# Four more row groups turned by VectorE in a linear-attention and mixture-of-experts kernel

## The chip, the cores and the metric

The kernel runs on one core of a Trainium2 chip. The metric is the device time of one execution in microseconds (us); the number to compare is the median of several runs. The core has a matrix engine (TensorE, PE in the profile; its weight loads are listed as PEld), a vector engine (VectorE, DVE), an activation engine (ScalarE, ACT), GpSimd (POOL) and SyncE (SP), which here does nothing but issue transfers. Sixteen DMA engines serve the transfer queues of SP, ACT and POOL.

## The reference

Two blocks follow each other, all in 32-bit floats. The first is lightning attention with decay; B = 4 sequences, 8 heads, 768 positions, 64 columns a head:

```python
for b in range(nb):                     # blocks of positions
    intra = einsum('bhic,bhjc->bhij', qb, kb) * Dmask
    intra = einsum('bhij,bhjd->bhid', intra, vb)
    inter = einsum('bhid,bhde->bhie', qb * lam_pow, kv_state)
    out[:, :, sl] = intra + inter
    kv_state = lam_block * kv_state + einsum('bhsd,bhse->bhde', kb * rev_pow, vb)
```

Its output becomes 3072 rows x of 512 columns. The second block sends each row to one of 8 experts:

```python
logits = x @ w_gate;  local = sigmoid(x @ w_local)
e = argmax(logits[s]) if s == 0 or local[s] < 0.5 else previous e of the sequence
out[s] = softmax(logits[s])[e] * (relu(x[s] @ w1[e]) @ w2[e])    # 512 -> 1024 -> 512
```

## The kernel before

**Attention steps.** Rows are handled in 24 steps of 128; step s is chunk s // 4 of sequence s % 4, so four steps make one group of 512 rows. Each step loads a 1 MB tile `inp` (q, k, v and k again; 768 KB in the last four steps) five steps ahead, in `loaded`. In the steps' loop PE runs `scores(s + 1)` (q against k into the PSUM tiles ps0 and ps1; DVE then multiplies by the mask into `sm`), `from_state(s)`, some router work, `mix(s)` (v against `sm`), and `update(s)` (new state). ACT copies the result of `mix` into `xc`, which holds the transposed rows of the current group of four steps. One matmul call in 32-bit floats shows in the trace as two matmuls and two weight loads; a transpose call shows as one of each.

**Scores.** For most steps `scores` cuts the 128 keys into two halves and leaves out the masked quarter: 16 calls. For the steps in `WIDE` all 128 keys are taken at once: 8 calls.

**Rows to memory.** The expert block gathers rows by index, so `xc` must go to the DRAM tile `x_dram` untransposed. There are two ways. `rows_of(s)`: four PE transposes into PSUM (pk1), one ACT copy into `xn`, one transfer of 256 KB, issued by ACT (by SP for the last). `turned_rows(s)`: one DVE transpose in blocks of 32 x 32 into a buffer of the group, and once the group's rows are there `group_out(k)` writes them with four SP transfers in pieces of 512 bytes. `TURNED` maps each step treated the second way to the step after whose work it is turned: steps 0 to 11, and 20, 21 and 22. Steps 12 to 19 and 23 use `rows_of`. The buffers of groups 0 to 4 are the two halves of the weight tile `w1t[1]` by turns; that of group 5 is a free `inp` buffer.

**Order.** PE, DVE, SP and POOL run in the order in which the code is written (`manual_schedule`); ACT's place is chosen by the framework. The transfers that SP and ACT issue take eight completion semaphores by turns, in an order that the framework works out; an issue waits until the earlier transfer on its semaphore has landed.

**Around the boundary.** In step 20 POOL multiplies the last query tile (`prepare(23)`, which needs `inp` 23) and then gathers the first two tiles of 128 rows, `ahead(0, 0)` and `ahead(1, 1)`; these read only the rows of groups 0 to 2. In step 23 `first_turned` transposes the first tile on PE (pr), and DVE copies it to `xtt[0]`. The second tile is turned by DVE (`flipped`) and ACT (`moved`). `hidden` and `output` are the expert layers: 64 and 16 matmuls of the trace. The weights of experts 0 and 1 are loaded during the last steps; `weights(g)` reads tile g's expert and loads it under a condition, into the buffer of tile g - 2. Five tiles are done so; after them come mostly pairs of tiles, with seven products instead of eight (`pair`).

Of the kernel before, what the change touches and what calls it, by code (L numbers as in the profile page):

```python
# [8 lines left out]
F32 = mybir.dt.float32  # L9
# [14 lines left out]
P = 128  # L24
B, H, S, DH = 4, 8, 768, 64
# [13 lines left out]
PARTS = [(0, 8), (8, NA), (NA, NT)]  # L39
LOADS = 6  # L40
QUARTERS = [16, 17, 18, 19]
WIDE = [3, 4, 5, 7, 9, 11]
TURNED = {**{r: r + 1 for r in range(3 * B)}, 11: 13, 20: 22, 21: 23, 22: 23}
WARM = 10
KA = -(-(NA * P - E * (P - 1)) // P)

# [19 lines left out]
def kernel(  # L66
# [175 lines left out]
    def mix(s):  # L242
        b, c = ORDER[s]
        sm, x = sms.pop(s), inp[s]
        vn = x[:, 2].rearrange("p (a u d) -> p a u d", u=2, d=DH)
        head, po = heads.pop(s), pos.pop(s)
        for a in range(A):
            for u in range(2):
                nc.tensor.matmul(head(a, u), lhsT=vn[:, a, u], rhs=sm[:, u, a],  # L249
                                 start=(not c and a < 2), stop=True, skip_group_check=True)  # L250
        for i in range(2):
            nc.scalar.copy(xc[:, i::2, b], po[i])
# [17 lines left out]
    def rows_of(s):  # L270
        px = pg.tile([P, DM], F32, name="pk1")
        for a in range(A):
            nc.tensor.transpose(px[:, P * a:P * a + P], xc[:, a, ORDER[s][0]], ident)
        if s + 1 < NS:
            xn = att.tile([P, DM], F32, name="xn", bufs=4)
        else:
            xn = xlast
        nc.scalar.copy(xn.rearrange("p (j d c) -> p j d c", j=4, c=QP), px.rearrange("p (d j c) -> p j d c", j=4, c=QP))


        queue = nc.scalar if s + 3 < NS else nc.sync
        queue.dma_start(out=x_dram[P * s:P * s + P, :], in_=xn)

    groups = {}

# [10 lines left out]

    def group_out(k):

        n = sum(r // B == k for r in TURNED)
        rows = x_dram[B * P * k:B * P * k + n * P, :]  # L300
        for j in range(4):
            nc.sync.dma_start(out=rows[:, P * j:P * j + P].rearrange("(i a) m -> a i m", a=QP),
                              in_=groups[k][QP * j:QP * j + QP, :n].rearrange("a b i m -> a (b i) m"))

    def gates(k):

        for d in range(DT):
            nc.tensor.matmul(pl[EP * d:EP * d + EP], lhsT=wgt[:, d], rhs=xc[:, d].rearrange("p b i -> p (b i)"),  # L308
                             start=True, stop=True, skip_group_check=True)
        lg = lgs[k] = rt.tile([P, B * P], F32, name="lg")  # L310
        nc.scalar.copy(lg, pl)
# [417 lines left out]
    def ahead(g, i):  # L729
        collect(xgt[i], *at(g))  # L730

    def first_turned():
        for d in range(DT):
            nc.tensor.transpose(pr[:, P * d:P * d + P], xgt[0][:, P * d:P * d + P], ident)
        nc.vector.tensor_copy(xtt[0].rearrange("p d i -> p (d i)"), pr)  # L735

    def flipped(xq, xg):

        nc.vector.transpose(xq, xg)  # L739
# [67 lines left out]
    with tc.manual_schedule(engines={PE, DVE, SP, POOL}):  # L807

        warm = pg.tile([P, A, P], F32, name="pk0")
        for _ in range(WARM):  # L810
            nc.tensor.matmul(warm[:, 0], lhsT=ident, rhs=ident, start=True, stop=True)
        masks_of_lam()
        nc.gpsimd.memset(wgt, 0.0)
        constants_1()

        for s in range(LOADS - 1):
            inp[s] = load.tile([P, 4, DM], F32, name="inp")
        for s, half in ((0, 0), (1, 0), (0, 1), (1, 1), *((s, half) for s in range(2, LOADS - 1) for half in range(2))):
            nc.sync.dma_start(out=inp[s][:, 2 * half:2 * half + 2], in_=qkv[s][:, 2 * half:2 * half + 2])
        for s in range(3):  # L820
            prepare(s)
        scores(0)
        nc.sync.dma_start(out=wgt[:, :, :E + 1], in_=wg)
        for s in range(NS):
            if s + LOADS - 1 < NS:
                loaded(s + LOADS - 1)
            if s + 3 < NS and s != 1:
                prepare(s + 3)
            if s in QUARTERS:
                j = QUARTERS.index(s)  # L830
                nc.sync.dma_start(out=w1t[0][:, j], in_=w1_src(0)[:, j])
            if s == NS - 4:
                nc.sync.dma_start(out=w2t[0], in_=w2_src(0))
                weights(0)
            if s == NS - 1:
                nc.sync.dma_start(out=w1t[1], in_=w1_src(1))
                nc.sync.dma_start(out=w2t[1], in_=w2_src(1))
            if s + 1 < NS and s not in (1, 2, 3, 4, 5):
                scores(s + 1)
            from_state(s)  # L840
            if s % B == 1 and s > B:
                logits(s // B - 1)
            if s == 5:
                scores(6)
            extra_work(s, 0)
            if s % B == 0 and s:
                gates(s // B - 1)
            mix(s)
            if s == 0:
                update(0)  # L850
                query_powers(0)
            if s in (1, 2, 3, 4):
                scores(s + 1)
            if s == 1:
                query_powers(1)
                prepare(4)
            if s:
                update(s)
            if s + 1 == NS:
                first_turned()  # L860
            if s > 1 and s - 1 not in TURNED:
                rows_of(s - 1)
            for r in [r for r in TURNED if TURNED[r] == s]:
                turned_rows(r)
                if r + 1 not in TURNED or r % B == B - 1:
                    group_out(r // B)
            extra_work(s, 1)
        x_ctx.close()
        act = ctx.enter_context(tc.tile_pool(name="act", bufs=2))
        w1t.append(act.tile([P, DT, F], F32, name="w1_2", bufs=1))  # L870
        w2t.append(act.tile([P, FT, DM], F32, name="w2_2", bufs=1))
        pools.append(act)

        pys.extend(pg.tile([P, DM], F32, name=f"pk{i}") for i in range(2))
        hq.update({(f, 1): act.tile([P, FT // 2, P], F32, name=f"h{f}1", bufs=1) for f in range(2)})
        xgh = act.tile([P, DM], F32, name="xgh", bufs=1)
        yt = act.tile([P, 2, DM], F32, name="y", bufs=1)
        xps = [act.tile([P, DT, P], F32, name=f"xp{i}", bufs=1) for i in range(3)]
        xs = act.tile([P, 3, DT // 2, P], F32, name="xs", bufs=1)
        s1 = act.tile([P, 3, DT // 2, F // 2], F32, name="s1", bufs=1)  # L880
        yl = s1[:, 0]
        s2 = act.tile([P, 3, FT // 2, DM // 2], F32, name="s2", bufs=1)
        hs = act.tile([P, 4, FT // 2, P], F32, name="hsum", bufs=1)
        part = act.tile([P, 3, FT // 2, P], F32, name="part", bufs=1)
        rest = act.tile([P, DM // 2], F32, name="rest", bufs=1)

        def finished(g):
            output(g % 2, g % 2)
            written(g, g % 2)

        def hiddens(g):
            hidden(g % 2, g % 2, 0)
            hidden(g % 2, g % 2, 1)


        xqs.extend((xlast, rt.tile([P, DM], F32, name="lg")))
        ahead(2, 0)
        xq = hq[1, 0].rearrange("p f i -> p (f i)")
        flipped(xq, xgt[1])
        ahead(3, 1)  # L900
        moved(xtt[1], xq, (0, 1))
        hidden(0, 0, 0)
        rows_of(NS - 1)
        weights(1)
        gates(NC - 1)
        moved(xtt[1], xq, (2, 3))
        hidden(0, 0, 1)
        by_slots(0, (2, 3, 4))
        logits(NC - 1)
        fresh_experts(2)  # L910
        flipped(xqs[1], xgt[0])
        ahead(4, 0)
        moved(xtt[0], xqs[1])
        finished(0)
        weights(2)
        along_sequences(2)
        flipped(xqs[0], xgt[1])
        hiddens(1)
        moved(xtt[1], xqs[0])
        experts_of(2)  # L920
        chances(2)
        flipped(xqs[1], xgt[0])
        finished(1)
        weights(3)
        ranks(2)
        masks(2)
        other_tiles()
        tokens_to_other_tiles()
        hiddens(2)
        moved(xtt[0], xqs[1])  # L930
        output(0, 0)
        weights(4)
        brought(1, (0, 1, 2, 3, 4))
        written(2, 0)
        hiddens(3)
        weights_of(KA, w_of(0), (1,))
        output(1, 1, range(FT // 2))
        by_slots(1, (0, 1, 2, 3, 4))
        output(1, 1, range(FT // 2, FT))
        written(3, 1)  # L940
# [417 lines left out]
```

## Time and profile before

| | |
|---|---|
| median of 3 runs | 447.33 us (446.29 to 447.91) |
| profiled execution | 447.0 us, of which the span in the trace is 445.3 us |
| PE busy | 427.9 us (96%) |
| DVE, ACT, POOL busy | 286.4, 195.0, 108.7 us |
| transfers | 124.84 MB, mean 280 GB/s |
| attention steps | 0 to 98.7 us, then experts |
| first expert matmul | 100.1 us |

Times in a trace count from the span's start. In a timeline line the columns are start, duration, engine, source line, operation, output and inputs, and in brackets the idle time before it and what ended it. "issue" means that the engine waited for nothing that the profile shows. In a wait line the numbers are the total, the count and the longest. The profiled execution is 0.3 us faster than the median.

### The profile page before, as it was taken

Reading aid. Unit: us, or ns where it says so; the run is one execution under the profiler, and the core shown is the slowest. Engines: PE = TensorE matmul, PEld = TensorE weight load, DVE = VectorE, ACT = ScalarE, POOL = GpSimd, SP = SyncE. Lnnn points to the kernel's source line nnn. Section 1 sums busy time; section 2 is a strip of 40 time slices with the busy share of each in tenths; the row PEclk is TensorE's granted clock in tenths of the full one; section 3 lists DMA queues with packets and bytes.
Section 4 is the critical chain, followed back from the end, with each engine's and each line's share of the span. In section 5 each row is a group of like instructions: output and inputs, shape, how many; then the busy total and the mean of one; then the engine's idle time right before and its main releaser. Section 6 shows DMA issues by size and latency. Waiting matters only on the chain.

```text
span 445.3 us, 10336 instructions
## 1 busy us (share of the span) xinstructions
PE 427.9 (96%) x4094; PEld 354.9 (80%) x4094; DVE 286.4 (64%) x564; ACT 195.0 (44%) x592; POOL 108.7 (24%) x120
## 2 busy tenths in 40 slices
PE   6999989889999999999999999999999999999993
PEld 6787777678667876978777999667899999898982
DVE  5767986882339949757372785100587879878661
ACT  4245555436455104663234456451455454565110
POOL 4495574321100042205121301200202021020101
PEclk9999999899999999999999999999999999999998
DMA  8999999979999899999993799996164828370101
GB/s 265 409 366 384 369 327 330 348 292 370 345 401 364 277 306 394 399 396 405 393 399 144 236 399 370 326 380 223 40 214 138 311 84 300 131 268 3 54 1 52
DMA packets 48352, 124.84 MB, mean 280 GB/s; under 512 B 3165, under 2 KB 10845, under 8 KB 46369
## 3 DMA queue, kind: packets, MB, share of 16 engines
q1 hardware_dynamic: 42624, 108.03, 66.5%
q0 software_dynamic: 4368, 13.90, 8.8%
q10 hardware_dynamic: 1296, 2.10, 1.3%
q8 instruction: 36, 0.59, 0.5%
q14 instruction: 28, 0.22, 0.2%
HBM read 124.02 MB, written 12.91 MB: 308 GB/s over the span
## 4 chain that ended last, share of the span: by engine, by line
PE 76%; DMA 11%; issue 6%; DVE 5%; POOLq 0%; POOL 0%; ACT 0%; DVEq 0%
PE ps L753 13%; PE pk L759 12%; PE ps L981 11%; PE pk L986 10%; DMA out_dram<-y,sidxp 6%; PE po L249 5%; PE po L981 5%; PE pl L986 4%; DMA w<-in_w_dram 4%; PE ps L209 3%; PE po L236 2%; PE pr L1142 2%; DVE sm L213 2%; PE pk L263 2%; PE pl L308 2%
## 5 line engine op out<-in xcount | busy, mean ns | idle before, releaser
L753 PEld LDWEIGHTS ps<-xt,w 128*128 128x128 f32 x512 | 58.2, 192 | 3.5 <-issue 2.3
L753 PE MATMUL ps<-xt,w 128*128 128x128 f32 x512 | 59.1, 276 | 0.8 <-DVE xt L735 0.8
L759 PE MATMUL pk<-w,h 128*128 128x512 f32 x128 | 56.5, 593 | 0.0
L759 PEld LDWEIGHTS pk<-w,h 128*128 128x128 f32 x128 | 23.6, 190 | 26.3 <-issue 25.6
L768 POOL DMA_INDIRECT out_dram<-y,sidx x14 | 14.0, 1001 | 105.4 <-DVE y L785 46.5
L725 POOL DMA_INDIRECT xg<-x_dram,gidx x25 | 25.8, 1031 | 55.5 <-DVE lg L739 34.1
L746 ACT COPY xp<-xlast 32x128 f32<-32x128 f32 x128 | 37.8, 295 | 1.7
L213 DVE TENSOR_TENSOR sm<-ps,mask 128x512 f32<-128x512 f32 x46 | 29.5, 682 | 9.6 <-PE ps L209 4.9
L755 ACT ACTIVATE h<-ps 128x512 f32<-128x512 f32 x16 | 9.6, 597 | 56.3 <-PE ps L753 56.3
L746 ACT COPY xp<-lg 32x128 f32<-32x128 f32 x112 | 33.0, 295 | 2.6
L785 DVE TENSOR_SCALAR y<-pk,gate 128x512 f32<-128x512 f32 x8 | 6.0, 744 | 42.1 <-PE pk L759 25.8
L178 POOL TENSOR_TENSOR qd<-inp,lamq 128x512 f32<-128x512 f32 x20 | 25.5, 1276 | 28.8 <-DMA inp<-in_qkv_dram 18.3
L981 PEld LDWEIGHTS ps<-xp,w 128*128 128x128 f32 x256 | 30.4, 192 | 2.1 <-issue 1.8
L981 PE MATMUL ps<-xp,w 128*128 128x128 f32 x256 | 31.4, 276 | 0.1
L981 PE MATMUL ps<-xs,s 128*128 128x128 f32 x256 | 31.2, 275 | 0.0
L986 PE MATMUL pk<-w,h 128*128 128x256 f32 x128 | 30.5, 381 | 0.0
L986 PE MATMUL pk<-s,hsum 128*128 128x256 f32 x128 | 30.3, 380 | 0.0
L249 PE MATMUL po<-sm,inp 128*64 128x128 f32 x384 | 28.0, 283 | 2.3 <-DVE sm L213 1.6
L249 PEld LDWEIGHTS po<-sm,inp 128*64 128x64 f32 x384 | 21.5, 139 | 10.6 <-issue 6.4
L981 PEld LDWEIGHTS ps<-xs,s 128*128 128x128 f32 x256 | 29.9, 192 | 0.0
L986 PEld LDWEIGHTS pk<-s,hsum 128*128 128x128 f32 x128 | 23.9, 190 | 3.3 <-DVE s L1069 0.2
L986 PEld LDWEIGHTS pk<-w,h 128*128 128x128 f32 x128 | 23.5, 190 | 3.4 <-issue 0.6
(282 smaller groups left out, 784.4 us busy)
## 6 DMA issues: line engine op xcount, KB each, us to landing
w<-in_w_dram SPq DMA_DIRECT2D x43, 2048.0 KB, 12.8
inp<-in_qkv_dram SPq DMA_DIRECT2D x15, 1024.0 KB, 10.9
inp<-in_qkv_dram SPq DMA_DIRECT2D x10, 512.0 KB, 7.9
x_dram<-w SPq DMA_DIRECT2D x12, 256.0 KB, 6.3
inp<-in_qkv_dram SPq DMA_DIRECT2D x4, 768.0 KB, 9.2
x_dram<-xn ACTq DMA_DIRECT2D x8, 256.0 KB, 6.7
w<-in_w_dram SPq DMA_DIRECT2D x4, 512.0 KB, 5.7
x_dram<-inp SPq DMA_DIRECT2D x4, 192.0 KB, 10.4
```

The source lines that it names most:

```text
L178: nc.gpsimd.tensor_tensor(qd, x[:, 0].rearrange("p (a i) -> p a i", i=P), lamq, ALU.mult)
L209: nc.tensor.matmul(ps[u][half, a, first:], lhsT=kt[rows, a, half], rhs=qt[rows, a, first:], start=True, stop=True, skip_group_check=True)
L213: nc.vector.tensor_tensor(sm[:, u], ps[u], mask[:, u], ALU.mult)
L249: nc.tensor.matmul(head(a, u), lhsT=vn[:, a, u], rhs=sm[:, u, a], start=(not c and a < 2), stop=True, skip_group_check=True)
L725: nc.gpsimd.indirect_dma_start(out=xg, out_offset=None, in_=x_dram[:n, :], in_offset=bass.IndirectOffsetOnAxis(ap=gidx[i][:, j:j + 1], axi ...
L746: copy(xt[QP * j:QP * j + QP, :, QP * k:QP * k + QP], blocks[QP * k:QP * k + QP, :, j])
L753: nc.tensor.matmul(ph[:, j], lhsT=w1t[w][:, d, P * f:P * f + P], rhs=xtt[i][:, d], start=(d == 0), stop=(d == DT - 1))
L755: nc.scalar.activation(hq[half, i], ph, ACT.Relu)
L759: nc.tensor.matmul(pys[i], lhsT=hq[f // 4, i][:, f % 4], rhs=w2t[w][:, f], start=(f == 0), stop=(f == FT - 1))
L768: apart(nc.gpsimd.indirect_dma_start(out=out, out_offset=bass.IndirectOffsetOnAxis(ap=sidx[i][:, j:j + 1], axis=0), in_=y, in_offset=None, ...
L981: nc.tensor.matmul(to[:, m], lhsT=a[:, k, P * m:P * m + P], rhs=b[:, k], start=(new and not m and not k), stop=(k == 1), skip_group_check= ...
L986: nc.tensor.matmul(to, lhsT=a[:, f], rhs=b[:, f], start=(new and not f), stop=(f == FT // 2 - 1), skip_group_check=True)
```

## The change

Steps 12 to 15 (the fourth group) and step 23 are turned by DVE as well. The turning of 12, 13 and 14 comes in step 15 and that of 15 in step 16, with a `group_out(3)` there. Steps 21 to 23 are turned after the steps' loop, behind the flip of the second tile, and `group_out(5)`, now of four rows' worth, comes behind `weights(1)` on SP. `first_turned` moves ahead of the last `mix`. Step 13 joins `WIDE`.

```diff
-WIDE = [3, 4, 5, 7, 9, 11]
-TURNED = {**{r: r + 1 for r in range(3 * B)}, 11: 13, 20: 22, 21: 23, 22: 23}
+WIDE = [3, 4, 5, 7, 9, 11, 13]
+TURNED = {**{r: r + 1 for r in range(4 * B)}, 11: 13, 12: 15, 13: 15, 20: 22}
@@ rows_of
-        if s + 1 < NS:
-            xn = att.tile([P, DM], F32, name="xn", bufs=4)
-        else:
-            xn = xlast
+        xn = att.tile([P, DM], F32, name="xn", bufs=4)
-        queue = nc.scalar if s + 3 < NS else nc.sync
-        queue.dma_start(out=x_dram[P * s:P * s + P, :], in_=xn)
+        nc.scalar.dma_start(out=x_dram[P * s:P * s + P, :], in_=xn)
@@ group_out
-        n = sum(r // B == k for r in TURNED)
-        rows = x_dram[B * P * k:B * P * k + n * P, :]
+        rows = x_dram[B * P * k:B * P * k + B * P, :]
         for j in range(4):
             nc.sync.dma_start(out=rows[:, P * j:P * j + P].rearrange("(i a) m -> a i m", a=QP),
-                              in_=groups[k][QP * j:QP * j + QP, :n].rearrange("a b i m -> a (b i) m"))
+                              in_=groups[k][QP * j:QP * j + QP].rearrange("a b i m -> a (b i) m"))
@@ the steps' loop
+            if s + 1 == NS:
+                first_turned()
             mix(s)
...
             if s:
                 update(s)
-            if s + 1 == NS:
-                first_turned()
-            if s > 1 and s - 1 not in TURNED:
+            if s > 1 and s - 1 not in TURNED and s < NS - 3:
                 rows_of(s - 1)
             for r in [r for r in TURNED if TURNED[r] == s]:
                 turned_rows(r)
-                if r + 1 not in TURNED or r % B == B - 1:
+                if r % B == B - 1:
                     group_out(r // B)
@@ after the loop
         ahead(2, 0)
         xq = hq[1, 0].rearrange("p f i -> p (f i)")
         flipped(xq, xgt[1])
+        for r in range(NS - 3, NS):
+            turned_rows(r)
         ahead(3, 1)
         moved(xtt[1], xq, (0, 1))
         hidden(0, 0, 0)
-        rows_of(NS - 1)
         weights(1)
+        group_out(NC - 1)
         gates(NC - 1)
```

## The prediction

> **What bounds the kernel now.** I began with the page's first part: is there an engine with no room?
>
> ```profile
> PE 427.9 (96%) x4094; PEld 354.9 (80%) x4094; DVE 286.4 (64%) x564; ACT 195.0 (44%) x592; POOL 108.7 (24%) x120
> ```
>
> PE is busy for all but 17 us, and the chain of waits runs along it almost unbroken from 100 us to the last pair. All edits lie ahead of or just behind the first expert matmul at 100.1 us, so the question is how much earlier PE gets there, and whether the experts then keep the lead. For that I read the timeline of PE in steps 13 to 23:
>
> ```profile
> 58.21 0.66 PE L273 MATMUL pk<-ident,xc 128*128 128x128 f32 x4
> 58.79 0.90 PE L209 MATMUL ps<-inp 64*64 64x128 f32 x32
> 59.51 0.49 PE L236 MATMUL po<-qd,kv 64*64 64x128 f32 x9
> 61.27 0.45 PE L236 MATMUL po<-qd,kv 64*64 64x128 f32 x7 [1.27 <-issue]
> ...
> 73.35 0.33 PE L209 MATMUL ps<-inp 64*64 64x64 f32 x3 [0.65 <-issue]
> ...
> 86.09 0.60 PE L209 MATMUL ps<-inp 64*64 64x64 f32 x18 [1.24 <-issue]
> ...
> 87.38 1.94 PE L308 MATMUL pl<-xc,wgt 128*32 128x512 f32 x8
> ```
>
> Two things: four transposes of `rows_of` move the next work by 0.58 us (58.21 to 58.79), and three gaps end by "issue", with no semaphore behind them. Counting the trace's PE instructions between the resumptions at 61.27, 73.35 and 86.09 gives 252 weight loads, 252 matmuls and 8 waits each time: exactly 512. The instruction queue (packets of 16 KB) has one at 59.08-60.03, 70.99-71.87 and 83.66-84.60, just ahead of each. PE is waiting for its program. Packets follow a stalled one after 4.98 and 4.96 us, and PE resumes some 1.25 us after a packet's end. Without stalls PE uses 256 instructions in about 5.4 us here, so it now runs near the fetch's own pace.
>
> Then DVE and POOL, who might hold the boundary:
>
> ```profile
> 73.60 1.29 DVE L213 TENSOR_TENSOR sm<-ps,mask 128x512 f32<-128x512 f32 x2 [1.84 <-PE ps L209]
> ...
> 99.38 0.69 DVE L735 COPY xt<-pr 128x512 f32<-128x512 f32 x1 [0.86 <-PE pr L734]
> 99.99 1.29 DVE L294 STREAM_TRANSPOSE inp<-xc 128x512 f32<-128x512 f32 x2
> ```
> ```profile
> 88.15 1.27 POOL L178 TENSOR_TENSOR qd<-inp,lamq 128x512 f32<-128x512 f32 x1 [2.51 <-DMA inp<-in_qkv_dram]
> 89.58 1.21 POOL L725 DMA_INDIRECT xg<-x_dram,gidx  x1 [0.17 <-DVE kd L498]
> ```
> ```profile
> 60.30 3.98 SPq L302 DMA_DIRECT2D x_dram<-w  x4
> ...
> 101.32 10.16 SPq L302 DMA_DIRECT2D x_dram<-inp  x4
> ```
>
> From 73.6 us DVE runs nearly without a break to 86 us (router work), and its next rest before `xt` is small. The first gather cannot start before `inp` 23 has landed (its completion event: 87.99) and POOL has multiplied it; it lands at 96.22. And SP spends 4 us on a `group_out` in the loop, 10 us on the one behind the weights.
>
> **What the skill says.** The Trainium skill, Runtime: NRT & Kernel Launch, Instruction fetch mechanics: the program comes in blocks of 16 KiB, 256 instructions, and fetching is mostly hidden. The trace confirms the blocks, not the hiding: 512 instructions between stalls of 0.65 to 1.27 us. TensorE: Matmul & The Clock Gate, What's actually happening: the clock is halved after an idle window of about 3.4 us. The trace has half clock for 3.41 us from 86.81, behind the third stall; that is why L308 takes 1.94 instead of 1.0 us. VectorE: DVE Perf Modes, The three transpose paths: DVE transposes 32 x 32 blocks only, so the placing of the blocks falls to `group_out`'s transfers, whose price I take from the trace.
>
> **The change part by part.**
>
> *Rows of 12 to 15 off PE.* 16 transposes: 4 x 0.58 = 2.3 us of PE time, 32 instructions. ACT loses four copies (585 ns each) and four issues (0.33 us); ACT had waits of 0.2 to 1.5 us throughout, so nothing follows from that.
>
> *Step 13 wide.* In the chain a wide `scores` takes 1.09 us, a halved one 0.81: +0.28 us. It issues 32 instructions fewer.
>
> *Fetch.* By step 17 PE has issued 64 instructions fewer at each point of the work. I walked the block ends (every 256 instructions; 54.9, 61.27, 67.2, 73.35 and so on before) with the rule "next packet 5.0 us after a stalled one's, or 6.25 us from crossing to use". PE reaches the end at 61.3 having done 0.9 us more work, that at 66.3 with 1.5 us, that at 71.3 with 2.9 us. So the lead after step 16 is about 2.9 us: the removed 2.0 us and some 0.9 of stalls.
>
> *DVE gets four transposes*, 0.70 us each by L294: 2.1 us in step 15, 0.7 in step 16. The first three end near 67.9 us and put `sm` of step 17 off to 69.1; `scores(18)`, which must wait for it because it writes the same PSUM, starts near 69.9. Hidden, by under a microsecond. The last is ahead of `sm` of step 18, which then starts near 71.6 instead of 73.60. It eats most of the 1.84 us rest. DVE's lead from there is thus 2.0, not 2.9 us, and `by_slots` of step 19, which already waits for DVE's `lane`, is held to that. The 0.90 us that DVE waited for PE ahead of `sm` of step 21 then goes too: 2.9 us at `sm` of step 23.
>
> *SP.* The loads of `inp` 22 and 23 now stand behind `group_out(3)`, which waits for the transpose near 72 us and takes 4 us as at 60.30: `inp` 22 goes out near 76 as before (75.92), `inp` 23 near 77 (78.65 before). The weight quarters, which waited 14.1 us in three places for transfers of `xn` on their semaphores, go out earlier, so `w2t[0]` ends near 95.5 instead of 98.81. The bytes ahead of `inp` 23 are about the same; I take its landing at 86 to 88 us, the gather's landing at 94 to 95.5.
>
> *First tile ahead of the last mix.* Before: mix, transposes (0.6), copy (0.7), matmul. Now `mix` (1.02 us) covers the copy. DVE does sm 23, `val` (0.49), one transpose (0.65) and the copy (0.69) without the 0.86 us rest: the copy ends near 96.3, the first expert matmul starts near 96.4 to 97, against 100.13: 3.1 to 3.7 us. The two transposes at 99.99 follow the second tile's flip now; that flip is earlier, and only `group_out(5)` waits for them.
>
> *Row 23 off PE.* 0.58 us between two `hidden` halves, all on the path.
>
> Sum: 3.3 + 0.58 = **3.9 us**; I take 3.8. Against the profiled execution that is 443.2 us (span 441.5); against the median, **443.5 us**. Ends of the unknown parts: the fetch between no gain (-0.9) and all its stalls gone (+1.0 more); the gather's landing between 93.5 and 97 (+0.4, -2.0); the half-clock window gone or met elsewhere (+0.5 to -1.7, mostly covered by the gather).
>
> **Do the experts keep the lead?** `weights(2)` must be in time for `hidden` of tile 2 at 131.7 (127.9 with the lead). Before it was issued at 115.41 and landed at 125.75. Now SP does `weights(1)` first, which waits until expert 1's 4 MB have landed (114.64 before; near 110 now), then `group_out(5)`. With the queue empty I give that 4 us, as in the loop: issue near 114.5, landing near 125, three us in hand. Later loads hang on PE's own progress and shift with it.
>
> **The rivals.**
>
> *Lead partly eaten at the boundary* (0.22). `inp` 23 lands at 88 or later, the gather at 96.2 or later, and PE, 3 us early, sits ahead of a `mix` that could have run. Then the matmul starts at 98 to 99: gain 1.7 to 2.8 us, 444.5 to 445.6; in the worst part under 1.3. For it: the 2.51 us wait in POOL's line. Against: SP is freed of the `xn` waits.
>
> *`weights(2)` late: slower* (0.10). If `group_out(5)` takes the 10.16 us of before, times 4/3 for four rows (13.5 us), then `weights(2)` goes out near 124.5, lands near 134.8, and PE waits 7 us: net 3 us slower, 450 us. It decides once that issue is later than 117.6 us. For it: the four issues on record, the first alone 4.75 us. Against: those came straight behind 4 MB of loads; in the loop it was 3.9 to 4.2 us.
>
> *The rows were hidden in the fetch* (0.08): if the program's arrival sets the pace, 64 instructions are worth 1.5 us at most, and with a stall moved to a worse place the total is within 1.3 us of before: about 446.3.
>
> **How the numbers follow.** Likeliest (0.60): 442.4 to 444.3, forecast 443.5. Faster by over 0.3% (1.3 us, about what a measurement can tell): 0.60 plus most of the first rival, 0.81. Within 0.3%: 0.09. Slower: 0.10. The range 441.9 to 446.4 takes in the first rival and the extra fetch gain, and leaves out the slow one.
>
> **What would show it.** After: L273 with 16 transposes instead of 36, L201 with 16 more matmuls; the transposes of `xg` (L734's counterpart) ahead of the last `mix`; the first expert matmul near 96.5 us; few or no "issue" gaps over 1 us in steps 14 to 20; the four issues of `group_out(5)` near 110 to 114 us; no DMA wait on PE near 128 us. I am wrong if the matmul starts after 99 us, or if a wait for weights stands before tile 2.

## The result and the profile after

The changed kernel takes **451.57 us** (median of 5 runs, 451.20 to 451.89) against 447.24 us for the kernel before (5 runs of the same comparison): ratio **1.0092** (95% interval 1.0070 to 1.0115). It is slower by 4.3 us, where the forecast was 443.5 us, faster. The profiled execution took 451.89 us, its span is 450.2 us. Line numbers below the edit are 4 or 5 lower than before: the transposes of the first tile are L729, `hidden` is L748, `output` L754, `group_out` L297. In all ratios a run over 1.5% above the fastest of its kernel is left out, so a ratio need not be the quotient of the two medians; this touches e3 alone, with five of its 20 runs (450.2 to 451.9 us).

First the page's first part, for what went away:

```profile
PE 426.8 (95%) x4058; PEld 354.2 (79%) x4058; DVE 291.4 (65%) x569; ACT 192.0 (43%) x587; POOL 108.3 (24%) x120
```

The edit is there: 36 matmuls fewer on PE (20 transposes of `rows_of`; step 13 has 32 small ones fewer and 16 larger ones more), five instructions more on DVE. PE's work falls by 1.1 us, the span rises by 4.9. So time was lost in waits. The waits of PE over the whole execution (total, count, longest):

```profile
PE pr L428 <- DVE mark L420: 3.0, 2, 1.8
PE pr L729 <- DMA xg<-x_dram,gidx: 2.7, 1, 2.7
PE po L236 <- ACT xc L252: 2.0, 2, 1.0
...
PE pr L444 <- DVE run L437: 1.3, 1, 1.3
```

The first is in the attention steps (0.2 us in the kernel before); in part it comes and goes by chance, as the last section shows. The second and the last are at the boundary, and both are new. The timeline of PE there (the bracket holds the idle time ahead of the line):

```profile
97.64 0.84 PE L236 MATMUL po<-qd,kv 64*64 64x128 f32 x16 [1.04 <-ACT xc L252]
101.23 1.11 PE L729 MATMUL pr<-ident,xg 128*128 128x128 f32 x4 [2.75 <-DMA xg<-x_dram,gidx]
102.27 1.98 PE L249 MATMUL po<-sm,inp 128*64 128x128 f32 x16
104.18 4.05 PE L748 MATMUL ps<-xt,w 128*128 128x128 f32 x32
...
120.83 7.41 PE L748 MATMUL ps<-xt,w 128*128 128x128 f32 x64
129.54 0.22 PE L444 MATMUL pr<-identb,run 4*128 4x4 bf16 x3 [1.30 <-DVE run L437]
```

The first tile's transposes stand ahead of the last `mix` and wait 2.75 us for the gather, with that `mix` (1.98 us here, 1.09 at full clock) behind them. The first expert matmul starts at 104.18, 4.05 us later than before. Then `hidden` of tile 1 ends at 128.24, and `output` cannot follow at once because `run`, by which the router's matmuls at L444 go, is late. What SP did in that time says why:

```profile
74.17 4.26 SPq L297 DMA_DIRECT2D x_dram<-w  x4
81.47 0.35 SPq L171 DMA_DIRECT2D inp<-in_qkv_dram  x1
82.37 0.35 SPq L826 DMA_DIRECT2D w<-in_w_dram  x1
87.87 0.33 SPq L171 DMA_DIRECT2D inp<-in_qkv_dram  x1
...
119.72 0.09 SPq L697 DMA_DIRECT2D w<-in_w_dram  x1
119.86 3.40 SPq L297 DMA_DIRECT2D x_dram<-inp  x4
124.64 0.41 SPq L696 DMA_DIRECT2D w<-in_w_dram  x1
```

`inp` 23 leaves SP at 87.87 instead of 78.65. And `group_out(5)`, behind `weights(1)` (L697, which waits until expert 1's weights are in), leaves at 119.86 instead of 101.32. DVE's timeline and the chain of waits show whom that stops:

```profile
127.24 0.75 DVE L780 TENSOR_SCALAR y<-pk,gate 128x512 f32<-128x512 f32 x1 [11.07 <-DMA x_dram<-inp]
```
```profile
104.89 14.81 DMA w<-in_w_dram
119.72 0.09 SPq L697
...
121.83 5.13 DMA x_dram<-inp
...
127.24 0.75 DVE y L780
...
128.48 1.01 DVE run L437
...
129.54 0.22 PE pr L444 x3
```

Between 104 and 129 us the chain that ended last is a weight transfer, SP, the rows' transfer and DVE; PE is not in it. `y` of tile 0, the first write into a buffer pool opened after the steps, waits for the rows of group 5 to land (126.97), and `run` is behind `y` on DVE. The trace has `y` wait for the semaphores of the transfers: for all eight in e6 and e11 (below), for seven in the kernel before, for five here. Why it does so is read from the code and not tested: `y` is in a new pool, opened where the pools of the steps were closed, and the rows are written from a buffer of one of those. In the kernel before, PE and DVE have:

```profile
109.79 7.03 PE L759 MATMUL pk<-w,h 128*128 128x512 f32 x16
```
```profile
116.98 0.75 DVE L785 TENSOR_SCALAR y<-pk,gate 128x512 f32<-128x512 f32 x1 [4.63 <-DMA x_dram<-inp]
```

The rows landed at 116.85, just after `output` of tile 0, which `y` needs as well, had ended (116.82): the wait was there, but it cost nothing. `run` was done at 119.21, well ahead of the end of `hidden` of tile 1 at 124.4 us, so nothing showed on PE.

### The profile page after: what moved, and what is told of

Its sections match the earlier page's. It is cut to its first block, busy times and chain, and to the rows that moved or that the text cites. A ratio compares the mean times of both kernels' runs of the same rounds, so it can differ in the third digit from the quotient of the medians.

```text
span 450.2 us, 10285 instructions
## 1 busy us (share of the span) xinstructions
PE 426.8 (95%) x4058; PEld 354.2 (79%) x4058; DVE 291.4 (65%) x569; ACT 192.0 (43%) x587; POOL 108.3 (24%) x120
## 4 chain that ended last, share of the span: by engine, by line
PE 66%; DMA 16%; DVE 9%; issue 6%; SPq 1%; POOLq 0%; POOL 0%; ACT 0%; DVEq 0%
PE ps L978 12%; PE pk L983 11%; PE pk L754 11%; PE ps L748 10%; DMA w<-in_w_dram 6%; DMA out_dram<-y,sidxp 6%; PE po L978 5%; PE pl L983 4%; PE po L249 3%; DVE sm L213 2%; PE pr L1139 2%; PE pr L1117 2%; PE ps L201 2%; DMA x_dram<-xn 1%; PE ps L209 1%
## 5 line engine op out<-in xcount | busy, mean ns | idle before, releaser
L748 PEld LDWEIGHTS ps<-xt,w 128*128 128x128 f32 x512 | 58.4, 192 | 2.8 <-issue 2.6
L748 PE MATMUL ps<-xt,w 128*128 128x128 f32 x512 | 59.3, 276 | 0.0
L754 PE MATMUL pk<-w,h 128*128 128x512 f32 x128 | 56.5, 593 | 0.0
L754 PEld LDWEIGHTS pk<-w,h 128*128 128x128 f32 x128 | 23.6, 190 | 26.3 <-issue 25.6
```

The source lines that it names most:

```text
L748: nc.tensor.matmul(ph[:, j], lhsT=w1t[w][:, d, P * f:P * f + P], rhs=xtt[i][:, d], start=(d == 0), stop=(d == DT - 1))
L754: nc.tensor.matmul(pys[i], lhsT=hq[f // 4, i][:, f % 4], rhs=w2t[w][:, f], start=(f == 0), stop=(f == FT - 1))
```

## The experiments

Two theories of the loss. **The rows' gate:** `group_out(5)` behind `weights(1)` fixes the time of `y`, `run` and so of `output` of tile 1, whatever PE does before. **The gather's gate:** `inp` 22 and 23 go out late, so the gather and the first expert matmul are late. Rivals: the turned rows cost DVE more than PE gains; `first_turned` in its new place or the wide step 13 does the harm; the loss is chance. Key times (us) of all profiled executions, by number (a profile is one run: that of e3 took 444.43 us, 3.1 us less than the kernel's median, that of e5 2.1 less, that of e4 2.3 more):

| kernel | median / before, ratio [95%] | first matmul | rows of group 5 land | `y` of tile 0 | `output` of tile 1 |
|---|---|---|---|---|---|
| before | | 100.13 | 116.85 | 116.98 | 124.50 |
| after | 451.57 / 447.24, 1.0092 [1.0070, 1.0115] | 104.18 | 126.97 | 127.24 | 129.69 |
| e1 | 452.14 / 446.27, 1.0124 [1.0077, 1.0170] | 97.68 | 124.69 | 124.97 | 127.43 |
| e2 | 449.80 / 446.27, 1.0084 [1.0060, 1.0109] | 103.16 | 123.10 | 123.22 | 127.10 |
| e3 | 447.55 / 446.27, 1.0004 [0.9978, 1.0030] | 96.84 | 119.94 | 120.06 | 122.62 |
| e4 | 448.26 / 446.27, 1.0046 [1.0022, 1.0069] | 100.41 | 123.97 | 124.24 | 126.69 |
| e5 | 449.51 / 446.59, 1.0072 [1.0048, 1.0095] | 99.19 | 122.70 | 122.82 | 125.27 |
| e6 | 443.51 / 446.59, 0.9931 [0.9902, 0.9960] | 99.45 | 114.47 | 115.80 | 123.39 |
| e7 | 451.99 / 446.59, 1.0128 [1.0060, 1.0195] | 102.05 | 121.10 | 121.23 | 128.26 |
| e8 | 445.82 / 446.59, 0.9983 [0.9957, 1.0010] | 99.74 | 118.33 | 118.46 | 124.11 |
| e9 | 445.99 / 446.47, 0.9993 [0.9975, 1.0010] | 100.86 | 120.82 | 120.95 | 124.79 |
| e10 | 445.97 / 446.47, 0.9997 [0.9974, 1.0020] | 100.62 | 119.53 | 119.66 | 125.00 |
| e11 | 445.72 / 446.47, 0.9973 [0.9954, 0.9993] | 99.22 | 114.03 | 115.54 | 123.13 |
| e12 | 451.46 / 446.47, 1.0101 [1.0075, 1.0127] | 101.34 | 126.17 | 126.45 | 128.90 |

### e1: the loads of inp 22 and 23 ahead of group_out(3)

```diff
-                if r % B == B - 1:
+                if r % B == B - 1 and r // B != 3:
                     group_out(r // B)
+            if s + LOADS == NS:        # step 18, behind loaded(s + LOADS - 1)
+                group_out(3)
```

> The changed kernel with one edit: group_out(3) is issued on SP behind the loads of inp 22 and 23 (in step 18) instead of ahead of them (end of step 16). Theory A (late input): in the changed kernel inp 23 landed at 92.60 us (87.99 before), so the first gather landed at 101.18 (96.22) and PE sat 2.75 us at first_turned. With the edit inp 23 lands by 88, the gather by 96.5, first expert matmul near 99.5 to 100.5 instead of 104.2; time about 447.5 (451.6 less 4). Rival B (DVE has no room): the lead was lost on DVE, which holds sm of step 23 to 97.6 us whatever the inputs do; then the first expert matmul cannot come before 99.7 and PE's wait at the gather turns into a wait for DVE; also about 447.5, but the idle before the first expert matmul is put down to DVE. Rival C (late rows of group 5 are all of it): no change, 451.5.

Measured: 452.14 us, no better than the changed kernel. PE's timeline has the whole early lead, and then the whole loss:

```profile
97.68 3.84 PE L748 MATMUL ps<-xt,w 128*128 128x128 f32 x32
...
114.12 7.41 PE L748 MATMUL ps<-xt,w 128*128 128x128 f32 x64
127.26 0.24 PE L444 MATMUL pr<-identb,run 4*128 4x4 bf16 x3 [5.73 <-DVE run L437]
```

The first expert matmul is 6.5 us earlier than in the changed kernel, and PE then waits 5.73 us. At 125.1 to 131.9 us the clock is halved, which takes 2.2 us more from `output` of tile 1 (9.26 us to `hidden` of tile 2 instead of 7.06). So the late gather is not what holds the total while the rows' gate stands.

### e2 and e3: group_out(5) ahead of weights(1), alone and with e1

```diff
+        group_out(NC - 1)
         weights(1)
-        group_out(NC - 1)
         gates(NC - 1)
```

> The changed kernel with one edit: group_out(5) is issued ahead of weights(1) on SP, as in the kernel before. Theory A2 (rows of group 5 landed at 126.5 us, and y of tile 0 and h of tile 1, which lie in the memory of the closed pools, waited for them: DVE 11.1 us, ACT 5.9 us, PE 1.3 us at the router matmuls): the wait of y for x_dram goes back to about 4.6 us, the step from the first to the second expert output on PE shrinks by 1.3 us; time about 450.2. Rival: DVE and ACT waits were covered, PE's 1.3 us came from elsewhere: 451.5. Second rival: weights(2) now goes out after 10 us of issues and is late for tile 2: 452 or more, with a DMA wait on PE near 135 us.

> Both edits of e1 and e2. If A and A2 are two separate causes they add: 451.6 - 4 - 1.3, about 446.2. If the two loads explain only part and DVE holds PE, about 447 to 448. If neither, 451.5.

In e2 PE no longer waits for `run`; the gather's gate is left (landing 101.51, first expert matmul 103.16), and the kernel is 0.84% slower than before. With both edits (e3) the loss is gone, but there is no gain: 1.0004 (0.3% slower by the medians of all runs), single runs from 443.2 to 451.9 us. Why they spread so far stays open; the profile is of one of the fastest. Its lines, of PE, SP and DVE, show what takes part of the lead even there:

```profile
115.15 7.38 PE L748 MATMUL ps<-xt,w 128*128 128x128 f32 x64 [1.80 <-DMA w<-in_w_dram]
```
```profile
103.64 10.14 SPq L297 DMA_DIRECT2D x_dram<-inp  x4
```
```profile
120.06 0.75 DVE L780 TENSOR_SCALAR y<-pk,gate 128x512 f32<-128x512 f32 x1 [11.44 <-DMA x_dram<-inp]
```

The four issues behind 4 MB of weights take 10.14 us again, and `hidden` of tile 1 waits 1.80 us for its weights. The two gates stand in series: lifting the gather's alone gave 1.0124, the rows' alone 1.0084, both 1.0004. Their gains must not be added: each alone gained little or nothing, both together 0.9%.

### e4 and e9: the tail alone; with group_out(5) ahead

Rows 12 to 15 go back to `rows_of` and step 13 is halved again (`WIDE` and `TURNED` up to group 2 as before); rows 21 to 23 stay behind the loop. e9 has e2's edit as well.

> The changed kernel with rows 12 to 15 back on PE (rows_of) and step 13 back to halved scores; what is left of the change is the end: first_turned ahead of the last mix, steps 21 to 23 turned after the loop, group_out(5) behind weights(1). Theory A: inp 23 and the gather come as before (88.0 and 96.2 us), so the end's own edits show: -0.6 us for row 23, about -0.5 for first_turned, +1.3 for the late group 5; about 447.4, near the kernel before. Rival (the end's edits are the loss): 450 to 452.

> e4 (rows 12 to 15 back on PE, step 13 halved, only the end of the change) with group_out(5) ahead of weights(1). If the 2.0 us that e4 cost against the kernel before are the late rows of group 5 (y of tile 0 at 124.2 us, PE's gap between tile 1's hidden and output 9.85 instead of 7.5 us), they go: gap 7.5 us, 445.5 to 446.3, at or just under the kernel before. Rival (turning 21 to 23 by DVE or the moved first_turned costs it): 448.

e4 is 0.46% slower with the first expert matmul on time (100.41): the rows land at 123.97, PE waits 2.28 us for `run` and runs at half clock after it (8.75 us from `output` of tile 1 to `hidden` of tile 2, 7.06 in the kernel before). e9: no difference from before. So the place of `group_out(5)` alone makes a slower kernel of an even one.

### e5: e2 with the four quarter loads of w1 all in step 19

```diff
-            if s in QUARTERS:
-                j = QUARTERS.index(s)
+            for j in range(4 if s == NS - 5 else 0):
                 nc.sync.dma_start(out=w1t[0][:, j], in_=w1_src(0)[:, j])
```

> The changed kernel with group_out(5) ahead of weights(1) (as in e2), and the four quarter loads of w1 issued together in step 19 instead of one each in steps 16 to 19. group_out(3) keeps its place ahead of the loads of inp 22 and 23; only the semaphores that these two wait on change: now those of inp 20 and of group_out(3)'s first transfer, no longer a quarter's and xn's of row 17. Theory A-semaphore (of the 9.2 us that inp 23 was late in issue, most was the wait for semaphores of transfers still in flight): inp 23 goes out near 82 and lands by 88, the gather by 97, first expert matmul near 99.5, time near e3's 447.5. Theory A-place (SP standing in group_out(3) is the cause): inp 23 still goes out after 85, the gather lands after 99, time near e2's 449.8.

The loads of `inp` keep their place behind `group_out(3)`, but the order in which semaphores are taken is another. SP's timeline:

```profile
71.71 8.14 SPq L297 DMA_DIRECT2D x_dram<-w  x4
79.95 1.30 SPq L171 DMA_DIRECT2D inp<-in_qkv_dram  x2
81.31 10.66 SPq L825 DMA_DIRECT2D w<-in_w_dram  x4
```

Although `group_out(3)` took 8.14 us, `inp` 23 went out by 81 us, and the gather landed at 96.64 instead of 101.51 in e2. In the changed kernel one view, SP's waits, has the line to match:

```profile
SPq L171 <- DMA x_dram<-xn: 5.1, 1, 5.1
```

So 5.1 of the 9.2 us by which `inp` 23 went out late were a semaphore last used for a transfer of `xn` (that of row 17, issued at 81.73, landed at 87.78), and not the queue place itself; `inp` 22 ahead of it had waited 2.9 us for a weight quarter in the same way. In the four profiles with this order on SP (after, e2, e7 and e12) `inp` 23 leaves 0.09 us after the landing of that `xn`. The time is no better than e2's (449.51): the weights now came late, and PE waited 2.0 us for expert 1's first layer.

### e6 and e11: group_out(5) between the two weight loads of expert 1

```diff
                 nc.sync.dma_start(out=w2t[0], in_=w2_src(0))     # step 20
+                nc.sync.dma_start(out=w1t[1], in_=w1_src(1))
                 weights(0)
...
-            if s == NS - 1:
-                nc.sync.dma_start(out=w1t[1], in_=w1_src(1))
-                nc.sync.dma_start(out=w2t[1], in_=w2_src(1))
...
             turned_rows(r)
+        group_out(NC - 1)
+        nc.sync.dma_start(out=w2t[1], in_=w2_src(1))
         ahead(3, 1)
         ...
         weights(1)
-        group_out(NC - 1)
```

These lines come on top of e1's edit. e11 is e6 with step 13 halved.

> e3 with SP's order at the boundary changed: w1 of expert 1 is loaded right behind w2 of expert 0 (ahead of weights(0)), then group_out(5), then w2 of expert 1, then weights(1). If the rest of the loss in e3 is that the rows of group 5 land at 119.9 (y of tile 0 waits for them until 120.06) and w1 of expert 1 at 115 (tile 1 could start at 113.1), both go: w1 lands near 108, group 5 near 110, tile 1's hidden starts 7 us behind tile 0's output; 2 to 3 us less than e3, 444.5 to 445.5, below the kernel before. Rival: DVE and POOL hold the steps ahead, and the boundary only moves the wait: 447.5 as e3.

> e6 with step 13 halved again. If the fetch paces these steps, undoing the wide scores costs 0.3 to 0.7 us against e6 (444); if PE's time does, it gains 0.3 us (443.2). A difference of over 1.3 us would mean that it acts through something else.

e6 beats both kernels: 443.51 us, ratio 0.9931. SP's and DVE's lines:

```profile
105.82 3.82 SPq L297 DMA_DIRECT2D x_dram<-inp  x4
109.68 2.26 SPq L898 DMA_DIRECT2D w<-in_w_dram  x1
```
```profile
115.80 0.75 DVE L780 TENSOR_SCALAR y<-pk,gate 128x512 f32<-128x512 f32 x1 [4.57 <-PE pk L754]
```

The issues take 3.82 us here, the rows are in (114.47) before `output` of tile 0 ends (115.70), and `y` waits for PE, not for a transfer: the gate is open. The edit also brings the first layer's weights of expert 1 in time: `hidden` of tile 1 starts at 115.89 without a wait; how much of the gain each of the two gives is not separated. `output` of tile 1 starts at 123.39, straight after `hidden`. The next gate is near: the weights of tile 2 land at 130.07, and PE begins with it at 130.45. e11, 0.9973, is some 0.4% slower than e6 (2.2 us, more than either reading allowed for), but the intervals overlap slightly; whether the wide step 13 helps stays open.

### e7, e8, e10: one part of the change alone in the kernel before

e7: rows 12 to 15 turned, `group_out(3)` at the end of step 16, nothing else. e8: `first_turned` ahead of the last `mix`, nothing else. e10: step 13 in `WIDE`, nothing else.

> The kernel before with only steps 12 to 15 turned by DVE (TURNED for them as in the changed kernel, group_out(3) at the end of step 16); step 13 halved, the end of the steps as before. Theory A: this part alone carries the late inp 22 and 23, so the gather lands near 101 and the first expert matmul comes near 103 to 104; but first_turned stands behind mix, so nothing runs later than the gather allows: 449 to 450. Rival (the loss needs first_turned ahead of the last mix): PE runs mix in the wait, 447 to 448. The prediction's own claim for this part was a gain of 2 us: 444.5.

> The kernel before with only first_turned moved ahead of the last mix. The gather lands at 96.2, PE is through from_state(23) near 97.7: no wait, and mix (1.0 us) covers DVE's copy: first expert matmul 0.3 to 0.8 us earlier, 445.6 to 446.2 against 446.3. Rival: in runs where the gather is late, PE waits with mix behind it: 446.5 to 447.

> The kernel before with only step 13 in WIDE. By PE's time +0.28 us, by the instruction fetch (32 instructions fewer) up to -0.7 us: 445.8 to 446.9, which a comparison may not tell from the kernel before. Rival: it shifts the order of the transfers' semaphores like the other parts and costs over 1.3 us.

e7 alone costs 1.3%. Its `group_out(5)` is in the old place; its wait on PE is the gather:

```profile
PE pr L734 <- DMA xg<-x_dram,gidx: 3.1, 1, 3.1
```

`inp` 23 goes out at 86.90 and the gather lands at 100.11. The kernel's time is 2 us above what was expected; one cost that was not counted is the clock, halved from 99.1 to 105.9 us, so that half a `hidden` takes 5.67 instead of 3.84 us:

```profile
102.05 5.67 PE L753 MATMUL ps<-xt,w 128*128 128x128 f32 x32 [0.78 <-DVE xt L735]
```

e8 and e10 do nothing that can be measured; in e8 the transposes wait 1.28 us for the gather (landed 98.08) in their new place too. So the harm came with the rows of group 3 and with `group_out(5)`; these two alone do none. What the new place of `first_turned` costs where the gather is as late as in the changed kernel was not run by itself.

### e12: the changed kernel again

> The changed kernel once more, for a second profile beside the others. Theory A and A2 (set by the program's order): inp 23 lands after 91, the first gather after 99.5, y of tile 0 starts within 0.3 us of the landing of group 5's rows, after 124 us; 451 to 452. The 1.7 us by which the first profile was behind at the 10th mix, ahead of every change, need not come again (theory: chance of when GpSimd's products meet DVE's small operations).

It repeats: 1.0101. In this profile the first expert matmul starts at 101.34, 2.8 us earlier than in the first one, and most of that is lost in the wait for `run`:

```profile
99.73 0.66 PE L729 MATMUL pr<-ident,xg 128*128 128x128 f32 x4 [0.30 <-DMA xg<-x_dram,gidx]
...
128.74 0.22 PE L444 MATMUL pr<-identb,run 4*128 4x4 bf16 x3 [3.55 <-DVE run L437]
```

The steps ahead of the change differed by chance; the time at which `output` of tile 1 may start did not by more than 0.8 us (128.90 and 129.69).

## Why the prediction was wrong

**Rows off PE: right in size on average, the part of the fetch not shown.** From `mix` of step 12 to that of step 17 the nine profiles with the rows on DVE take 18.97 us on average (17.16 to 20.70), the five without 21.79 (20.77 to 23.32): a lead of 2.8 us (2.9 forecast). Of this the forecast gave 0.9 us to stalls of the fetch. The first profile of the changed kernel has no wait by "issue" on PE above 0.4 us in these steps, but the second, of the same program (e12), has the stalls again:

```profile
75.22 0.55 PE L249 MATMUL po<-sm,inp 128*64 128x128 f32 x6 [1.56 <-issue]
...
81.41 0.60 PE L209 MATMUL ps<-inp 64*64 64x64 f32 x18 [0.65 <-issue]
...
88.47 0.43 PE L236 MATMUL po<-qd,kv 64*64 64x128 f32 x3 [2.39 <-issue]
```

They are 256 and 254 of PE's instructions apart, one block each, while e10, with the rows on PE, has none above 0.4 us. So how the stalls fall differs from run to run, and that the change removed any is not shown. Some readings behind the forecast's walk were also off. By the 512 instructions between stalls, 256 take about 5.7 us and not 5.4; PE resumed 1.24, 1.48 and 1.49 us after a packet's end and not each time some 1.25; and the 5.0 us between packets do not hold in the changed kernel, where one starts 3.61 us after another (78.95 and 82.56).

**The lead kept on DVE: mis-sized.** The forecast carried 2.9 us to `sm` of step 23. From `mix` of step 17 to that of step 22 the same nine profiles need 1.55 us more than the five (21.96 against 20.41): 1.3 us are left on average. In the kernel before, DVE rested 0.94, 1.84 and 0.90 us ahead of `sm`; in the changed kernel one such rest of 0.28 us is left, so the room that was to hide the transposes was used up. But the nine spread from 19.42 to 25.02, and the three longest (e2, e5, e12) have 3.41 us of half clock in this stretch (as the kernel before has), so DVE is not shown to be the whole cause.

**SP and the gather: wrong.** The step "the weight quarters go out earlier; `inp` 23 near 77" failed. Forecast: issue near 77, landing 86 to 88, gather 94 to 95.5. Measured: 87.87, 92.60 and 101.18. In effect it took the semaphores' order as unchanged but for the `xn` transfers removed. With them gone the loads took other semaphores, and `inp` 23 came to wait for the `xn` of row 17 (e5). The first rival, a gather at 96.2 or later, was in the right place; it priced the gather a few microseconds too low.

**The first tile ahead of the mix: right only with a timely gather.** Where the gather landed early, the order does what was said: 97.68 in e1 and 96.84 in e3, against a forecast of 96.4 to 97. With a late gather it can turn against the kernel, since the last `mix` could have run in the 2.75 us.

**group_out(5): the step that decided.** The prediction said that "only `group_out(5)` waits for" the turned rows and looked for the next victim at `weights(2)`. It never asked who waits for `group_out(5)`. A first sign is in the kernel before: `y` of tile 0 came 0.13 us after the landing of the rows. There `output` of tile 0 had ended at the same time, so that trace alone does not settle it; the others do. `y` came between 0.12 and 0.28 us after it in before, after, e1 to e5, e7 to e10 and e12. From `y` to `output` of tile 1 it takes 2.45 us (127.24 to 129.69), and that `output` was due at 124.50, or 120.7 with the lead of 3.8: so `y` could be as late as about 118.25. With the forecast's own time of issue (114.5), the measured 3.4 us for the issue and 3.7 us to the landing, the rows are in at 121.6: too late by over 3 us, which eats most of the gain. With the real issue, 119.86, they were 8.7 us too late. The slower rival had the place (`group_out(5)` behind `weights(1)`) and nearly the total (450), but neither the victim nor the price: the issues took 3.40 us and not 13.5, close to the forecast's 4, and PE did not wait for `weights(2)`. These went out at 124.64, later than the 117.6 that was to decide, and landed at 134.49; tile 2 began at 136.75, itself late by the rows' gate. In the kernel before it had begun at 131.56, so these weights were the next gate behind that of the rows. The rival's total was near by accident.

**Against the profile before.** The span grew by 4.9 us. At `mix` of step 12, ahead of all that the change does but the wide step 13, the changed kernel is already 2.16 us late, which in e12 is 0.04 us, so it comes and goes from run to run. To `mix` of step 18 it gains 2.41, to that of 22 it loses 0.30, and to the first expert matmul it loses 4.00; sum 4.05. `output` of tile 1 is 5.19 us late. In e12, without the late start, the matmul is 1.21 us late and `output` of tile 1 4.40. The rows' gate makes a late one of both.

## What to carry to other kernels

A write that is moved behind a wait has readers and also buffers that are freed by it: look in the trace of before for every instruction that starts just after that write lands, though it costs nothing there, and work out how late it may be. A gate that hangs on transfers cannot be outrun by the engine behind it, so an earlier gain is worth only what the latest gate behind it leaves; lift the last gate first, then judge the rest. Where transfers share completion semaphores by turns, taking some transfers away changes what all later ones wait for.

## What was not expected of the hardware

**Small DVE operations stretched by GpSimd.** Ahead of all that the change does, `mix` of step 12 starts at 55.12 us in the first profile of the changed kernel and at 53.00 in the second (e12). It is one program; among what differs ahead of it are three router operations on DVE. The first fence is DVE in the first profile, the second POOL in the same one, the third DVE in e12:

```profile
43.06 1.11 DVE L417 TENSOR_TENSOR top<-lt,mx 128x64 f32<-128x64 f32 x1
44.20 0.97 DVE L418 TENSOR_TENSOR top<-top,down 128x64 f32<-128x64 f32 x1
```
```profile
42.82 1.27 POOL L178 TENSOR_TENSOR qd<-inp,lamq 128x512 f32<-128x512 f32 x1 [0.21 <-DMA inp<-in_qkv_dram]
44.05 1.04 POOL L181 TENSOR_TENSOR kd<-inp,rev 128x512 f32<-128x512 f32 x1
```
```profile
42.57 0.22 DVE L417 TENSOR_TENSOR top<-lt,mx 128x64 f32<-128x64 f32 x1
42.83 0.22 DVE L418 TENSOR_TENSOR top<-top,down 128x64 f32<-128x64 f32 x1
```

With the third, `mark` at L420 (1.12 against 0.17 us), it is 3.20 us against 0.61. Each long one ends within 0.1 us of the end of a product on POOL; in e12 POOL sat waiting for `inp` from 42.12 to 43.91, with no product under way. The Trainium skill, SBUF — State Buffer, SBUF: two separate sides, says that a DVE operation with two inputs from SBUF and a GpSimd operation that reads SBUF take a shared pair of ports as an exclusive lock, and the other is fully blocked. The trace fits this, and shows it as a longer instruction, not as a wait. Of small DVE operations, with one input or two, that take over 0.35 us more than is usual for them there are 8 in before (5.9 us in excess), 11 in the first profile of the changed kernel (8.8 us), 6 in e12 (5.1 us). All but one of those 25 end within 0.12 us of the end of a product on POOL. No experiment took the products away on purpose; the cause rests on this pair of runs and on the coincidences. Nor do these three operations explain every start: in before they take 1.94 us in all, and its `mix` of step 12 starts at 52.96.

**The half clock after short pauses.** In the changed kernel PE's clock was halved from 101.2 to 104.6 us, after a wait of 2.75 us: the four transposes took 1.11 instead of 0.66 us, the `mix` 1.98 instead of 1.09. That is shorter than the some 3.4 us of idleness that the Trainium skill (TensorE: Matmul & The Clock Gate, What's actually happening) gives and the prediction used; here the measurement decides. In this profile the changes of the clock are 95.57, 3.41 and 341.33 us apart, whole multiples of 3.41 us. In the 3.41 us ahead of the halving PE was busy for 0.66 us; in the kernel before, ahead of 86.81 us, for 1.91 us, with no pause above 1.24 us. A wait of 1.81 us at 63.09 in the changed kernel halved nothing. So a stretch that is idle only in part can halve the clock, but these runs give no fixed limit.
